# Decode step of an adaLN block: the last quarter of the gate modulation's weights as 112 rows in four pieces of 28 on partitions 0 to 27, instead of 100 rows in five pieces of 20 on partitions 32 to 51

## The chip, the cores and the metric

The kernel runs on one core of one Trainium2 chip. The time is device microseconds of one execution of the whole program; three runs of the kernel before gave 696.67, 697.14 and 704.57 us, median 697.14 us. Times inside an execution come from one profiled execution and count from its first instruction.

## The reference

One token for each of two sequences (B = 2) goes through a block whose shifts, scales and gates come from a condition vector `c` (2 x 512). Attention has 32 heads of width 128 over a cache of 4096 keys and values in float32; the feed-forward part is 512 -> 1376 -> 512 with Mish.

```python
mod = (_silu(c) @ w_mod).reshape(c.shape[0], 6, 1, -1)
sa, ca, ga, sb, cb, gb = (mod[:, 0], mod[:, 1], mod[:, 2], mod[:, 3], mod[:, 4], mod[:, 5])
h = _layernorm(x, axis=-1) * (1 + ca) + sa
x = x + ga * _A_ref(h, A_k_cache, A_v_cache, A_wq, A_wo)
h = _layernorm(x, axis=-1) * (1 + cb) + sb
x = x + gb * _B_ref(h, B_w1, B_b1, B_w2)
```

The change concerns `gb`, the sixth modulation, called m5 in the kernel: `silu(c)` (2 x 512) times the last 512 x 512 block of `w_mod`. It is needed only for the last product of the kernel.

## The kernel before

All of the cache and all weights, some 297 MB, are read once. The host lays them out as a list of "loads", each at most 128 partitions x 64 KB, in the order in which they are used (`stream`). `load(n)` puts load n into one of three rotating 64 KB-wide tiles ("room") with one or more transfers, all issued from the SP queue; `used(...)` marks a part as consumed and issues the next load once everything in the room's former load is consumed. SP's transfers take eight completion semaphores (DMAHW0 to DMAHW7) in turn, and SP's order shows that a transfer waits for the one eight places ahead of it.

For each head VectorE multiplies the keys by q and sums (lines 334 and 337), ScalarE takes exponentials, TensorE multiplies by the values. After the last head comes a tail that TensorE leads: the last values, the output projection, the second normalisation, modulations 4, 3 and 5, the two feed-forward products, and the store. In the tail every engine works through its instructions in the order of the code. The last two loads are:

- load 34: modulation 4's weights and the last head's values (3072 KB, 1024 KB, 1024 KB), then the pieces of m5, `m5p`, as four small transfers (line 154).
- load 35, seven transfers: modulation 3's weights with the first half of `w1` (2400 KB), the second half of `w1` (1376 KB), **m5's first 384 rows together with the first chunk of `w2` (1024 KB)**, then the other chunks of `w2` (1280, 768, 256 and 256 KB).

The 512 contraction rows of m5 are dealt out three ways. Rows 0 to 383 are three full blocks of 128 rows (`wm5`), in the third transfer of load 35. `PIECES` pieces of `ROWS` rows come as `m5p` with load 34: the pieces lie side by side in the free dimension, so that one partition's row holds one row of each piece, and the four transfers take every fourth row. The rest, 28 rows, lies in the padding of `w2`'s first chunk from partition 96 on (`REST0`). The matching entries of `silu(c)` are in `ct5`, one column group for each piece.

`terms5` lists the products in this order: the pieces, the three full blocks, the rest. `modulation_5(lo, hi)` issues terms lo to hi - 1, four matmuls each (one for each 128 columns), which all add into `gps`. It is called four times in the tail, among other matmuls:

```python
    modulation_5(0, 2)
...
    modulation_5(2, 4)
...
    modulation_5(4, PIECES)
...
    modulation_5(PIECES, len(terms5))
```

The third call stands between the transposition of the normalised x (`h2ps`, line 253, copied to `h2t` by VectorE) and the first feed-forward product (`w1ps`, line 560). The fourth stands behind the matmuls that add the hidden values into `fps` (line 575). `busy(n)` issues matmuls whose result is not used. VectorE then forms Mish from `fps` (lines 588 to 595), TensorE multiplies by `w2` (`yps`, line 604), and VectorE multiplies by `gb`, adds x (lines 611 and 612) and SP stores.

Of the kernel before, what the change touches and what calls it, by code (L numbers as in the profile page):

```python
# [13 lines left out]
P = 128  # L14
WIDTHS = (384, 384, 352, 256)
CHUNKS = [(g, j) for j in range(3) for g in range(4) if WIDTHS[g] > P * j]
ROW0, ROWS, STEP = 32, 20, 4
PIECES = 5
M5 = 3
REST0 = WIDTHS[2] - 2 * P  # L20
REST = 512 - P * M5 - ROWS * PIECES
HEADS = 32
HC = 4
BIG = 8192
# [3 lines left out]
    "k": BIG, "v": HALF, "wq": W, "wo": W, "m01": 2 * W, "m2": W, "m3": W, "m4": W, "m5": 512 * M5,  # L28
    "m5p": 512 * PIECES, "w1": 4 * sum(WIDTHS), "w2": 512 * len(CHUNKS),
}  # L30
# [5 lines left out]
def stream():  # L36


    order, n_v = [], 0
    for h in range(1, HEADS):  # L40
        order.append(("k", h))
        if h % HC == HC - 1 and HC < h < HEADS - 1:
            c = (h + 1) // HC
            order.append([("wq", c), ("wo", c - 2)])
        if h not in AHEAD:
            order += [("v", n_v, 0), ("v", n_v, 1)]
            n_v += 1
    order = [x if isinstance(x, list) else [x] for x in order]

    def size(x):  # L50
        return sum(SIZES[key[0]] for key in x)

    loads = [[([("m01", 0), ("wq", 0), ("wq", 1)], (4 * W,)), ([("k", 0)], (BIG,))]]
    for _ in range(1, HEADS):
        row = []
        while size(row) < ROW:
            room = ROW - size(row)
            row += order.pop(next(i for i, x in enumerate(order) if size(x) <= room))
        loads.append([(row, (ROW,))])
    last = [("v", h, i) for h in range(HEADS - 4, HEADS) for i in range(2)]  # L60
    assert order == [[key] for key in last[:2]], order
    loads += [
        [(last[:2] + [("wo", 6), ("wo", 7), ("m2", 0)], (BIG + 3 * W,))],
        [(last[2:4], (BIG,)), (last[4:6], (BIG,))],
        [([("m4", 0)] + last[6:], (W + HALF, W, W)), ([("m5p", 0)], (512 * PIECES,))],
        [
            ([("m3", 0), ("w1", 0)], (W + 2 * sum(WIDTHS), 2 * sum(WIDTHS))),
            ([("m5", 0), ("w2", 0)], (512 * (M5 + 1), 5 * 512, 3 * 512, 512, 512)),
        ],
    ]  # L70
    return loads
# [3 lines left out]
def kernel(  # L75
# [17 lines left out]
    nc = tc.nc  # L93
# [13 lines left out]
    NCH = len(CHUNKS)  # L107
    NP5 = PIECES + 1

# [14 lines left out]
    def take(t, keys):  # L124
        lo = 0
        for key in keys:
            kind, n = key[:2]
            part = t[:, lo : lo + SIZES[kind]]
            lo += SIZES[kind]
            if kind == "k":  # L130
                k_t[n] = part.rearrange("p (j d) -> p j d", d=DH)
            elif kind == "v":
                v_t[n, key[2]] = part.rearrange("p (c n) -> p c n", n=512)
            elif kind in ("wq", "wo"):
                (wq_t if kind == "wq" else wo_t)[n] = part.rearrange("p (k n) -> p k n", k=G)
            else:
                w_t[kind] = part.rearrange("p (k n) -> p k n", k={"w2": NCH, "m5": M5, "m5p": PIECES}.get(kind, G))

    w_t = {}
    done = set()  # L140

    def load(n):

        t = kvp.tile([P, ROW], F32, tag="room", name=f"room{n}", bufs=3)
        lo = 0
        for keys, srcs in loads[n]:
            take(t[:, lo:], keys)
            for src in srcs:
                dst = t[:, lo : lo + src.shape[-1]]
                if src.shape[0] == P:  # L150
                    nc.sync.dma_start(out=dst, in_=src)  # L151
                else:
                    for i in range(STEP):
                        nc.sync.dma_start(out=dst[ROW0 + i : ROW0 + ROWS : STEP], in_=src[i::STEP])
                lo += src.shape[-1]

    loaded = 0

    def used(*keys):
# [26 lines left out]
        out=fold, in_=ident.rearrange("p (g r) -> p r g", g=G), axis=AX.X, op=ALU.add  # L186
# [3 lines left out]
        out=mean_w, in0=fold[:, None, :].to_broadcast([P, G, R]), scalar1=1.0 / D, scalar2=None, op0=ALU.mult  # L190
# [4 lines left out]
        out=half, in_=ident.rearrange("p (b r) -> p r b", b=B), axis=AX.X, op=ALU.add  # L195
# [14 lines left out]
    ct5 = const.tile([P, NP5, R], F32, name="ct5")  # L210
# [99 lines left out]
    def busy(n, bank=1):  # L310

        for lo in range(0, n, 2):
            cols = P * min(2, n - lo)
            nc.tensor.matmul(ov[bank][:, :cols], lhsT=ident, rhs=e_t[0].rearrange("p c m -> p (c m)")[:, :cols], start=True, stop=True)  # L314
# [129 lines left out]
    for h in range(H):  # L444
# [38 lines left out]
        out=ct5[:, :, ::TB],  # L483
# [29 lines left out]
    wm3, wm5 = w_t["m3"], w_t["m5"]  # L513
    w1_t, w2_t = w_t["w1"], w_t["w2"]
    gps = ov[1 - N % 2][:, :P]
    rows5, rest5 = slice(ROW0, ROW0 + ROWS), slice(REST0, REST0 + REST)
    terms5 = [(ct5[rows5, n, :], w_t["m5p"][rows5, n, :]) for n in range(PIECES)]
    terms5 += [(ct[:, k, :], wm5[:, k, :]) for k in range(M5)]
    terms5.append((ct5[rest5, PIECES, :], w2_t[rest5, 0, :]))

    def modulation_5(lo, hi):
        for n in range(lo, hi):
            c, w = terms5[n]
            for g in range(G):
                nc.tensor.matmul(
                    gps[R * g : R * (g + 1)], lhsT=c, rhs=w[:, P * g : P * (g + 1)],
                    start=(n == 0), stop=(n == len(terms5) - 1),
                )
# [21 lines left out]
    nc.vector.tensor_copy(h2t[:, :, ::TB], h2ps)  # L550

    busy(1)
    modulation_5(4, PIECES)
    hq_pad = work.tile([P, 512], F32, tag="o", name="hq_pad")
    nc.gpsimd.memset(hq_pad[:, : NJ * P], 0.0)
    w1ps = wide_ps("w1ps")
    for k in range(G):
        lo = 0
# [9 lines left out]
    lo = 0  # L568
    for g in reversed(range(G)):
# [3 lines left out]
        lo = hi  # L573
    for j in range(NJ):
# [5 lines left out]
            stop=(j == NJ - 1),  # L580
            skip_group_check=True,
        )
    modulation_5(PIECES, len(terms5))
    busy(2)
    f = const.tile([P, 3, NJ * G, B], F32, name="f")
    hid = fps.rearrange("p (n b) -> p n b", b=B)
# [13 lines left out]
    for n in range(NCH):  # L600
        i = (n - 1) % NCH
# [15 lines left out]
def _lay_out(np, a):  # L617


    def rows(w):  # L620

        return w.reshape(-1, P, w.shape[-1]).transpose(1, 0, 2)

    def q_rows(v):

        return v.reshape(2, 4, P).transpose(1, 0, 2).reshape(8, P)

    B, H, S, DH = a["A_k_cache"].shape
    kv = {
        kind: a[n].reshape(B, H, P // B, -1).transpose(1, 0, 2, 3).reshape(H, P, -1)  # L630
        for kind, n in (("k", "A_k_cache"), ("v", "A_v_cache"))
    }
    wq = rows(a["A_wq"]).reshape(P, 4, 8, 512).transpose(2, 0, 1, 3).reshape(8, P, -1)
    wo = a["A_wo"].reshape(8, 4, P, 512).transpose(0, 2, 1, 3).reshape(8, P, -1)
    wm = rows(a["w_mod"])
    w1 = rows(a["B_w1"])
    starts = np.cumsum((0,) + WIDTHS)
    b1c = np.zeros((P, 12 + 2 * (PIECES + 1)), a["B_b1"].dtype)
    m5 = a["w_mod"][:, 512 * 5 :]
    m5p = np.zeros((P, PIECES, 512), m5.dtype)  # L640
    for n in range(PIECES + 1):
        f0 = P * M5 + ROWS * n
        to, size = (ROW0, ROWS) if n < PIECES else (REST0, REST)
        b1c[to : to + size, 12 + 2 * n : 14 + 2 * n] = a["c"].reshape(2, 512)[:, f0 : f0 + size].T
        if n < PIECES:
            m5p[to : to + size, n] = m5[f0 : f0 + size]
    w2 = np.zeros((P, len(CHUNKS), 512), a["B_w2"].dtype)
    for n, (g, j) in enumerate(CHUNKS):
        f0 = starts[g] + P * j
        f1 = min(f0 + P, starts[g + 1])  # L650
        b1c[: f1 - f0, n] = a["B_b1"][f0:f1]
        w2[: f1 - f0, (n + 1) % len(CHUNKS)] = a["B_w2"][f0:f1]
    w2[REST0 : REST0 + REST, 0] = m5[512 - REST :]

    pieces = {**kv, "wq": wq, "wo": wo, "m01": [wm[:, :, :1024]], "w1": [w1], "w2": [w2], "m5p": [m5p], "m5": [rows(m5)[:, :M5]]}
    for n in (2, 3, 4):
        pieces[f"m{n}"] = [wm[:, :, 512 * n : 512 * (n + 1)]]
    def piece(kind, n, part=None):
        row = pieces[kind][n].reshape(P, -1)
        return row if part is None else row[:, HALF * part : HALF * (part + 1)]  # L660

    arrays = {
        "head": np.stack([q_rows(a["c"]), q_rows(a["A_x"])], axis=1),
        "b1c": b1c,
    }
    for n, parts in enumerate(stream()):
        for i, (keys, widths) in enumerate(parts):
            row = np.concatenate([piece(*key) for key in keys], axis=1)
            cuts = np.split(row, np.cumsum(widths)[:-1], axis=1)
            for j, t in enumerate(cuts):  # L670
                arrays[f"load{n}_{i}_{j}"] = np.ascontiguousarray(t[ROW0 : ROW0 + ROWS] if keys == [("m5p", 0)] else t)
    return arrays


# [26 lines left out]
```

## Time and profile before

| what | value |
|---|---|
| times of three runs | 697.14, 696.67, 704.57 us |
| profiled execution, span from first to last instruction | 695.1 us |
| median of the runs less that span | 2.0 us |
| VectorE busy | 588.2 us (85%) |
| TensorE busy (matmul) | 290.5 us (42%) |
| ScalarE busy | 44.2 us (6%) |
| HBM read | 297.17 MB, 428 GB/s over the span |
| chain that ended last | DMA 67%, VectorE 30%, TensorE 2% |

The profiled execution is not one of the three timed runs; its own time is known only as its span, 695.1 us. The page gives busy time by engine and 40 slices of the span, the chain of work that ended last, groups of instructions and transfers. The timeline names for each instruction or run of equal instructions its start, its length, and in brackets how long the engine had been idle before it and who ended that. A line such as "1024.0 KB, 14.5" under transfers means that a transfer of that size landed 14.5 us after SP began to issue it. "PEclk" is the granted clock of TensorE as a share of full speed.

### The profile page before, as it was taken

To read this page: it belongs to the slowest core of one execution; us is meant where nothing else is said; L and a number is where in the kernel's file an instruction comes from. 1 tells how busy PE (TensorE), PEld (TensorE's weight loads), DVE (VectorE), ACT (ScalarE), POOL (GpSimd) and SP (SyncE) were. 2 spreads that over 40 slices of the span, in tenths; PEclk is the share of its full clock that TensorE was granted. 3 is DMA by queue.
4 is the path that set the end of the run, shared out by engine and by line. 5 is a ranking of instruction groups with operands and counts; after the bars stand their busy time and mean duration, and the time that the engine had idled before them with its cause. 6 is when DMAs were issued, how large, how long until landed. Compare 5 with 4: busy or idle time off the path is not lost.

```text
span 695.1 us, 4042 instructions
## 1 busy us (share of the span) xinstructions
PE 290.5 (42%) x1696; PEld 109.5 (16%) x1696; DVE 588.2 (85%) x223; ACT 44.2 (6%) x169; POOL 4.4 (1%) x20
## 2 busy tenths in 40 slices
PE   3603334335135625225242806235324425134887
PEld 1201011001002201101110301011101111001345
DVE  3599989999999999999999999999999999899002
ACT  1000000000000000000000000000000010000011
POOL 2000000000000000000000000000000000000000
PEclk9955655668575567666575565656585657656899
DMA  9999999999999999999999999999999999999997
GB/s 382 464 422 422 422 431 471 419 423 430 426 457 430 423 434 427 437 445 423 430 437 426 446 430 426 437 431 441 430 426 424 449 434 437 427 421 429 426 418 302
DMA packets 6986, 297.49 MB, mean 428 GB/s; under 512 B 924, under 2 KB 1060, under 8 KB 1444
## 3 DMA queue, kind: packets, MB, share of 16 engines
q1 hardware_dynamic: 6808, 297.22, 99.1%
q8 instruction: 13, 0.21, 0.1%
q10 hardware_dynamic: 160, 0.02, 0.0%
q14 instruction: 5, 0.04, 0.0%
HBM read 297.17 MB, written 0.07 MB: 428 GB/s over the span
## 4 chain that ended last, share of the span: by engine, by line
DMA 67%; DVE 30%; PE 2%; SPq 0%; issue 0%; ACT 0%; DVEq 0%
DMA room<-in_load 67%; DVE room L334 15%; DVE s L337 15%; PE qps L307 1%; PE modps L263 1%; SPq L151 0%; DVE m L350 0%; DVE hcw L296 0%; PE hps L253 0%; ACT q L308 0%; PE yps L604 0%; DVE y L611 0%; DVE hq L287 0%; DVE hq L286 0%; DVE y L612 0%
## 5 line engine op out<-in xcount | busy, mean ns | idle before, releaser
L334 DVE TENSOR_TENSOR room<-room,q 128x8192 f32<-128x8192 f32 x32 | 278.1, 8692 | 46.4 <-DMA room<-in_load 39.1
L337 DVE TENSOR_REDUCE s<-room 128x64 f32<-128x8192 f32 x32 | 277.9, 8684 | 0.4 <-DVE m L350 0.3
L375 PE MATMUL ov<-room,e 128*32 128x512 f32 x1024 | 170.6, 820 | 69.3 <-ACT e L353 39.8
L346 PE MATMUL mt<-d,same 128*128 128x64 f32 x64 | 19.0, 393 | 197.4 <-DVE d L344 197.4
L375 PEld LDWEIGHTS ov<-room,e 128*32 128x32 f32 x1024 | 38.4, 143 | 173.6 <-issue 125.2
L353 ACT ACTIVATE e<-s,m 64x64 f32<-64x64 f32 x64 | 22.1, 345 | 552.1 <-DVE m L350 551.3
L346 PEld LDWEIGHTS mt<-d,same 128*128 128x128 f32 x64 | 13.7, 267 | 226.3 <-DVE d L344 179.1
L307 PE MATMUL qps<-room,hcw 128*128 128x512 f32 x64 | 46.8, 902 | 4.4 <-DMA room<-in_load 3.6
L361 PE MATMUL l<-l,ones 128*128 128x8 f32 x16 | 4.6, 358 | 76.1 <-ACT e L353 76.1
L398 PE MATMUL otp<-pick,o 128*128 128x8 f32 (+2 forms) x72 | 14.4, 328 | 36.3 <-ACT o L390 34.9
L307 PEld LDWEIGHTS qps<-room,hcw 128*128 128x128 f32 x64 | 18.2, 297 | 28.0 <-issue 22.4
L398 PEld LDWEIGHTS otp<-pick,o 128*128 128x128 f32 x72 | 13.6, 282 | 45.3 <-ACT o L390 45.2
L390 DVE COPY o<-ov 128x256 f32<-128x256 f32 x1 | 0.4, 424 | 23.1 <-ACT o L390 23.1
L361 PEld LDWEIGHTS l<-l,ones 128*128 128x128 f32 x16 | 3.8, 297 | 77.5 <-ACT e L353 77.5
L350 DVE TENSOR_REDUCE m<-mt 128x1 f32<-128x64 f32 x32 | 7.0, 218 | 6.6 <-PE mt L346 6.6
L406 PE MATMUL att<-room,ot 128*32 128x512 f32 x62 | 10.2, 718 | 5.2 <-DMA room<-in_load 4.7
L353 ACT ACTIVATION_READ_ACCUMULATOR e<-s,m 64x1 f32 x64 | 11.8, 185 | 0.0
L344 DVE TENSOR_SCALAR d<-half,m 128x64 f32<-128x64 f32 x32 | 8.1, 254 | 1.1
L314 PE MATMUL ov<-e,ident 128*128 128x256 f32 (+1 forms) x36 | 8.5, 372 | 0.0
L342 DVE TENSOR_REDUCE m<-s 128x1 f32<-128x64 f32 x32 | 7.0, 217 | 0.9
L263 PE MATMUL modps<-room,ct 128*32 128x128 f32 (+1 forms) x128 | 7.0, 364 | 1.4 <-DMA room<-in_load 1.4
L390 ACT COPY o<-ov 128x512 f32<-128x512 f32 (+1 forms) x9 | 5.0, 561 | 27.3 <-PE ov L375 27.2
(107 smaller groups left out, 70.8 us busy)
## 6 DMA issues: line engine op xcount, KB each, us to landing
room<-in_load SPq DMA_DIRECT2D x4, 4096.0 KB, 25.1
room<-in_load SPq DMA_DIRECT2D x1, 7168.0 KB
room<-in_load SPq DMA_DIRECT2D x1, 3072.0 KB, 26.2
room<-in_load SPq DMA_DIRECT2D x3, 1024.0 KB, 28.3
room<-in_load SPq DMA_DIRECT2D x1, 2400.0 KB, 13.9
room<-in_load SPq DMA_DIRECT2D x1, 1376.0 KB, 14.5
room<-in_load SPq DMA_DIRECT2D x1, 1280.0 KB, 15.1
room<-in_load SPq DMA_DIRECT2D x1, 768.0 KB
```

Source lines behind the costliest of these rows:

```text
L263: nc.tensor.matmul(ps[R * g : R * (g + 1)], lhsT=ct[:, k, :], rhs=t[:, k, :].rearrange("p (m n) -> p m n", m=n)[:, :, P * g : P * (g + 1)] ...
L307: nc.tensor.matmul(ps, lhsT=hcw[:, k, :], rhs=wq_t[ch][:, k, :], start=(k == 0), stop=(k == G - 1))
L314: nc.tensor.matmul(ov[bank][:, :cols], lhsT=ident, rhs=e_t[0].rearrange("p c m -> p (c m)")[:, :cols], start=True, stop=True)
L334: nc.vector.tensor_tensor(out=k_t[h], in0=k_t[h], in1=qv, op=ALU.mult)
L337: nc.vector.tensor_reduce(out=s_t[h], in_=k_t[h], axis=AX.X, op=ALU.add)
L344: nc.vector.tensor_scalar(out=d, in0=half, scalar1=m_t[h][:, 0:1], scalar2=None, op0=ALU.mult)
L346: nc.tensor.matmul(mps[h], lhsT=same, rhs=d, start=True, stop=True)
L353: nc.scalar.activation(e_t[i][own_b, :, M * i + 4 * b : M * i + 4 * b + 4], s_t[h][own_b].rearrange("p (c m) -> p c m", m=4), AF.Exp, bias ...
L361: nc.tensor.matmul(lps[n], lhsT=ones, rhs=sum_t[n % 2], start=True, stop=True)
L375: nc.tensor.matmul(ov[bank][R * g : R * (g + 1), :], lhsT=e_t[h % HC][:, NB // 2 * part + c, :], rhs=v_t[h, part][:, c, :], start=(first a ...
L398: nc.tensor.matmul(tps[:, x], lhsT=o_t[m], rhs=pick_t[n][:, m, x], start=(m == 0), stop=(m == 3),)
L406: nc.tensor.matmul(att[R * i : R * (i + 1), :], lhsT=ot_t[n % 2][:, i, :], rhs=wo_t[n][:, i, :], start=(n == 0), stop=(n == H // HC - (2 i ...
```

## The change: what it does

There are four pieces of 28 rows instead of five of 20. They lie on partitions 0 to 27 instead of 32 to 51. Each of the four transfers now takes seven rows of 8 KB (4 x 512 floats) instead of five rows of 10 KB, so 112 rows and 224 KB come with load 34 instead of 100 rows and 200 KB. The rest is 16 rows instead of 28, in the same place in `w2`'s padding. The third and fourth calls of `modulation_5` now split the list of terms at `PIECES + 1`, which is 5 as `PIECES` was before.

```diff
-ROW0, ROWS, STEP = 32, 20, 4
-PIECES = 5
+STEP = 4
+PIECES, ROWS = 4, 28
...
-REST = 512 - P * M5 - ROWS * PIECES
+REST = 512 - P * M5 - PIECES * ROWS
...
-                dst = t[:, lo : lo + src.shape[-1]]
-                if src.shape[0] == P:
+                rows, width = src.shape
+                dst = t[:rows, lo : lo + width]
+                if rows == P:
                     nc.sync.dma_start(out=dst, in_=src)
                 else:
                     for i in range(STEP):
-                        nc.sync.dma_start(out=dst[ROW0 + i : ROW0 + ROWS : STEP], in_=src[i::STEP])
-                lo += src.shape[-1]
+                        nc.sync.dma_start(out=dst[i::STEP], in_=src[i::STEP])
+                lo += width
...
-    rows5, rest5 = slice(ROW0, ROW0 + ROWS), slice(REST0, REST0 + REST)
-    terms5 = [(ct5[rows5, n, :], w_t["m5p"][rows5, n, :]) for n in range(PIECES)]
+    rest5 = slice(REST0, REST0 + REST)
+    terms5 = [(ct5[:ROWS, n, :], w_t["m5p"][:ROWS, n, :]) for n in range(PIECES)]
     terms5 += [(ct[:, k, :], wm5[:, k, :]) for k in range(M5)]
     terms5.append((ct5[rest5, PIECES, :], w2_t[rest5, 0, :]))
...
     busy(1)
-    modulation_5(4, PIECES)
+    modulation_5(4, PIECES + 1)
     hq_pad = work.tile([P, 512], F32, tag="o", name="hq_pad")
...
-    modulation_5(PIECES, len(terms5))
+    modulation_5(PIECES + 1, len(terms5))
     busy(2)
...
-    m5p = np.zeros((P, PIECES, 512), m5.dtype)
+    m5p, f0 = np.zeros((P, PIECES + 1, 512), m5.dtype), P * M5
     for n in range(PIECES + 1):
-        f0 = P * M5 + ROWS * n
-        to, size = (ROW0, ROWS) if n < PIECES else (REST0, REST)
+        to, size = (REST0, REST) if n == PIECES else (0, ROWS)
         b1c[to : to + size, 12 + 2 * n : 14 + 2 * n] = a["c"].reshape(2, 512)[:, f0 : f0 + size].T
-        if n < PIECES:
-            m5p[to : to + size, n] = m5[f0 : f0 + size]
+        m5p[to : to + size, n] = m5[f0 : f0 + size]
+        f0 += size
```

Lines below the changed part of `load` stand one line further down after the change (604 becomes 605). How the instructions stand is shown at three places. On TensorE in the tail, between the transposition and the first feed-forward product (`room_1227` is load 34, `room_1356` load 35; the name in brackets is what an instruction waits for), before:

```order
L253 MATMUL h2ps<-ident,hq 128x8 [waits DVE_49]
L314 MATMUL ov_110<-e_160,ident 128x128
L525 MATMUL ov_109<-room_1227,ct_104 32x128 x4
L560 MATMUL w1ps<-room_1356,h2t 32x384 [waits DVE_49,Activation_49]
```

and with the change:

```order
L254 MATMUL h2ps<-ident,hq 128x8 [waits DVE_49]
L315 MATMUL ov_110<-e_160,ident 128x128
L526 MATMUL ov_109<-room_1356,ct 32x128 [waits DMAHW7_49]
L526 MATMUL ov_109<-room_1356,ct 32x128 x3
L561 MATMUL w1ps<-room_1356,h2t 32x384 [waits DVE_49,Activation_49]
```

The four matmuls of the fifth piece, which read load 34, are gone from this place; the four of the first full block stand there, read load 35 and wait for a transfer, DMAHW7. Behind `fps`, in the same queue, before:

```order
L575 MATMUL fps<-ident,hq_pad 128x8 [waits Activation_49]
L525 MATMUL ov_109<-room_1356,ct 32x128 [waits DMAHW7_49]
L525 MATMUL ov_109<-room_1356,ct 32x128 x11
L525 MATMUL ov_109<-room_1356,ct_104 32x128 x4
L314 MATMUL ov_110<-e_160,ident 128x256
L604 MATMUL yps<-room_1356,actt 32x128 [waits DVE_49,PE_49]
```

and with the change:

```order
L576 MATMUL fps<-ident,hq_pad 128x8 [waits Activation_49]
L526 MATMUL ov_109<-room_1356,ct 32x128 x8
L526 MATMUL ov_109<-room_1356,ct_104 32x128 x4
L315 MATMUL ov_110<-e_160,ident 128x256
L605 MATMUL yps<-room_1356,actt 32x128 [waits DVE_49,PE_49]
```

Four matmuls fewer stand there, and the wait for DMAHW7 has moved to the place above. On SP, the pieces and what follows them, before:

```order
L154 DMA room34_1227<-in_load34_1_0 5x2560 x2
L154 DMA room34_1227<-in_load34_1_0 5x2560 [waits DMAHW3_49]
L154 DMA room34_1227<-in_load34_1_0 5x2560 [waits DMAHW4_49]
L151 DMA room35_1356<-in_load35_0_0 128x4800 [waits DMAHW5_49,PE_49]
L151 DMA room35_1356<-in_load35_0_1 128x2752 [waits DMAHW6_49]
L151 DMA room35_1356<-in_load35_1_0 128x2048 [waits DMAHW7_49]
```

and with the change:

```order
L155 DMA room34_1227<-in_load34_1_0 7x2048 x2
L155 DMA room34_1227<-in_load34_1_0 7x2048 [waits DMAHW3_49]
L155 DMA room34_1227<-in_load34_1_0 7x2048 [waits DMAHW4_49]
L152 DMA room35_1356<-in_load35_0_0 128x4800 [waits DMAHW5_49,PE_49]
L152 DMA room35_1356<-in_load35_0_1 128x2752 [waits DMAHW6_49]
L152 DMA room35_1356<-in_load35_1_0 128x2048 [waits DMAHW7_49]
```

Only the shape of the four small transfers has changed. The last row is the transfer of m5's full blocks; it takes DMAHW7, for which TensorE waits above.

More of the change, by code (lines that the diff above doesn't have):

```diff
@@ L652, in _lay_out @@
         w2[: f1 - f0, (n + 1) % len(CHUNKS)] = a["B_w2"][f0:f1]
-    w2[REST0 : REST0 + REST, 0] = m5[512 - REST :]
-    pieces = {**kv, "wq": wq, "wo": wo, "m01": [wm[:, :, :1024]], "w1": [w1], "w2": [w2], "m5p": [m5p], "m5": [rows(m5)[:, :M5]]}
+    w2[REST0 : REST0 + REST, 0] = m5p[REST0 : REST0 + REST, -1]
+    pieces = {**kv, "wq": wq, "wo": wo, "m01": [wm[:, :, :1024]], "w1": [w1], "w2": [w2], "m5p": [m5p[:, :-1]], "m5": [rows(m5)[:, :M5]]}
     for n in (2, 3, 4):
@@ L670, in _lay_out @@
             for j, t in enumerate(cuts):
-                arrays[f"load{n}_{i}_{j}"] = np.ascontiguousarray(t[ROW0 : ROW0 + ROWS] if keys == [("m5p", 0)] else t)
+                arrays[f"load{n}_{i}_{j}"] = np.ascontiguousarray(t[:ROWS] if keys == [("m5p", 0)] else t)
     return arrays
```

## The prediction

> **What bounds the kernel now.** I read the page first, for the share of each resource.
>
> ```profile
> span 695.1 us, 4042 instructions
> DMA 67%; DVE 30%; PE 2%; SPq 0%; issue 0%; ACT 0%; DVEq 0%
> HBM read 297.17 MB, written 0.07 MB: 428 GB/s over the span
> ```
>
> The transfers run from end to end at 428 GB/s. VectorE's 30% of the chain are only the places where SP waits for a free room while earlier loads are still in flight. The change touches nothing until the last load, so all it can move is the end. There I read the chain of waits in order of time:
>
> ```profile
> 675.51 16.84 DMA room<-in_load
> 692.35 0.04 issue
> 692.39 0.47 PE yps L604 x8
> 692.88 0.30 DVE y L611
> ```
>
> The kernel ends when the last transfer of load 35 lands (692.35); after it come eight matmul passes, two steps of VectorE and the store. So TensorE's tail is not the bound now. How near it is to being the bound is what decides this change, and the timeline of the tail shows it:
>
> ```profile
> 682.64 0.47 PE L314 MATMUL ov<-e,ident 128*128 128x128 f32 x2
> 682.83 0.17 DVE L550 COPY h2t<-h2ps 128x8 f32<-128x8 f32 x1 [0.86 <-PE h2ps L253]
> 683.04 0.42 PE L525 MATMUL ov<-room,ct 20*32 20x128 f32 x8
> 683.39 2.78 PE L560 MATMUL w1ps<-room,h2t 128*32 128x384 f32 x32
> 686.73 0.84 PE L575 MATMUL fps<-ident,hq_pad 128*128 128x8 f32 x6 [0.56 <-ACT hq_pad L572]
> 687.49 1.21 PE L525 MATMUL ov<-room,ct 128*32 128x128 f32 x32
> 688.63 0.70 PE L314 MATMUL ov<-e,ident 128*128 128x256 f32 x2
> 688.93 0.20 DVE L595 TENSOR_TENSOR actt<-f 128x22 f32<-128x22 f32 x1
> 689.27 1.52 PE L604 MATMUL yps<-room,actt 96*32 96x128 f32 x48
> 691.13 1.08 PE L604 MATMUL yps<-room,actt 128*32 128x128 f32 x32 [0.34 <-DMA room<-in_load]
> 692.39 0.43 PE L604 MATMUL yps<-room,actt 128*32 128x128 f32 x8 [0.17 <-DMA room<-in_load]
> ```
>
> A matmul of the program appears as two passes (x8 for four). `yps` waits for transfers only 0.34 + 0.17 us in all. TensorE is thus about half a microsecond ahead of the transfers, and a delay beyond that anywhere from `w1ps` on reaches the end nearly in full.
>
> **The change, part by part.**
>
> *The moved term.* The third call of `modulation_5` issues term 4. That was the fifth piece, which came with load 34; now it is the first full block, whose weights are in the third transfer of load 35 (1024 KB). The order of the changed kernel has the wait for that transfer there. When it lands:
>
> ```profile
> room<-in_load SPq DMA_DIRECT2D x1, 1024.0 KB, 14.5
> 671.64 0.33 SPq L151 DMA_DIRECT2D room<-in_load  x1
> ```
>
> 671.64 + 14.5 = 686.14. That matmuls start at once after a landing is seen at load 35's first transfer, issued at 666.46 and landed 13.9 later, at 680.36, with modulation 3 starting at 680.40:
>
> ```profile
> room<-in_load SPq DMA_DIRECT2D x1, 2400.0 KB, 13.9
> 666.46 0.35 SPq L151 DMA_DIRECT2D room<-in_load  x1
> 680.40 1.08 PE L263 MATMUL modps<-room,ct 128*32 128x128 f32 x32 [0.24 <-DMA room<-in_load]
> ```
>
> So TensorE, which today runs this place at 683.04, would stand until 686.14 + 0.04 = 686.18. Everything behind it in its queue stands too: `w1ps`, `fps`, `yps`. ScalarE's `hq_pad` copies and VectorE's Mish wait for those. `h2t` is ready at 683.00 and no longer sets anything.
>
> *The pieces' transfers.* They are 25 KB more in total, 0.06 us at 428 GB/s. What counts is how they lie on the DMA engines, which no row shows: the page lists the four transfers without a landing.
>
> ```profile
> room<-in_load SPq DMA_DIRECT2D x4, 50.0 KB
> ```
>
> Bounds: 428 GB/s over 16 engines is 26.8 GB/s for one. If each transfer puts one row on each of five engines now and on each of seven then, an engine that carries pieces today gets 4 x 8 KB instead of 4 x 10 KB, 1.22 us instead of 1.53, and is 0.3 us earlier with all that follows; two engines that carry none today become 1.2 us later. A transfer lands with its slowest engine, so load 35's landings move by -0.3 (the slowest carries pieces today) to +1.2 us (the slowest is one of the two). I take -0.3: today's extra 1.5 us lie on a few engines while all other transfers load all engines alike, so the last one is likeliest among those. The Trainium skill, "DMA: Bandwidth & Descriptors", section "Why a DMA increments its semaphore by 16 and not by 1", has a transfer run on the largest number of engines up to 16 that divides its slowest dimension: five rows on five engines, seven on seven, the lowest-numbered; no row here shows it, and by it the two cases above are the only ones. SP issues the pieces in the same places with the same waits, and load 35's later transfers queue behind many microseconds of data, so their issue costs nothing; if the cover went, 0.3 us each.
>
> *The sum at TensorE's present pace.* Release at 686.18 - 0.3 = 685.88. The four moved matmuls take 683.39 - 683.04 = 0.35, so `w1ps` starts at 686.23, 2.84 later than now. From `w1ps` to `yps` it is 689.27 - 683.39 = 5.88 us; in it are now four matmuls fewer (8 of 32 passes of 1.21 us, 0.3 us), but they lay beside Mish, which ends with line 595 at 689.13, so I take 0 off. `yps` starts at 692.11. By then the last transfer has landed (692.35 - 0.3 = 692.05), and its 88 passes run without waits: 1.52 + 1.08 + 0.43 = 3.03, to 695.14 instead of 692.82. That is +2.3 us. If the landings moved by +1.2 instead it would be +3.8.
>
> *The clock.* The new wait is 685.88 - 683.11 = 2.8 us of idle TensorE. In consecutive stretches of 3.41 us the profile shows what idle time does to the granted clock (the number behind the count):
>
> ```profile
> core 0: us, PE busy (x), PEclk, DMA share, GB/s
> 649.44:652.86 3.42, 1.62 (x19) 1.00 1.02 429
> 652.86:656.27 3.41, 3.41 (x20) 0.50 0.99 425
> 656.27:659.68 3.41, 3.41 (x23) 1.00 0.90 387
> 669.92:673.34 3.42, 2.34 (x20) 1.00 1.05 435
> 673.34:676.75 3.41, 2.54 (x26) 1.00 1.01 433
> 683.57:686.99 3.42, 2.86 (x35) 1.00 1.00 413
> ```
>
> A stretch with 1.62 us of work (1.8 idle) is followed by one at half clock, a stretch with 2.34 is not (1.00 in the row behind it). With the change 683.57 to 686.99 would hold 1.1 us of work: the next stretch is granted half. I assume that the stretches' position is not tied to the program. An idle of 2.8 us is split so that neither part reaches 1.8 in (1.8 - 1.0) / 3.4, about a quarter of the positions. What half clock costs, by the values' matmuls:
>
> ```profile
> 652.90:656.20 3.30, 3.30 (x20) 0.50 0.96 410
> 662.80:666.40 3.60, 3.60 (x32) 1.00 0.97 414
> ```
>
> 165 ns for a pass instead of 112, times 1.47. A slow stretch of 3.4 us lies at most on 3.4 us of `w1ps`, which then loses 3.4 x (1 - 1/1.47) = 1.1 us; where it begins earlier or later it meets idle time or the small steps, and I estimate 0.6. So 0.6 to 1.1 in three of four positions; I take 0.9. The rule in the Trainium skill, "TensorE: Matmul & The Clock Gate", section "Part 1: The HAM clock gate", halves the clock after a whole idle window of about 3.4 us. By that rule the 2.8 us would not halve it, and the sum would stay at +2.3 (rival D); this trace's 649.44 row, half idle and followed by 0.50, speaks against it, so I go by the row.
>
> *The rest.*
>
> ```profile
> 675.80 0.42 DVE L390 COPY o<-ov 128x256 f32<-128x256 f32 x1 [23.06 <-ACT o L390]
> ```
>
> Matmuls on 28 instead of 20 rows, two columns less in the small steps on `c5` before the tail, the other partitions: TensorE's passes last as long for 20 rows as for 128 (rows at 683.04 and 687.49), and behind the `c5` steps VectorE has nothing to do for 23 us. Nothing.
>
> **Total:** 2.3 + 0.9 = +3.2 us, from a span of 695.1 to 698.3. The runs' median is 697.14, 2.0 above the span; I keep that difference: 697.14 + 3.2 = 700.3 us.
>
> **The rivals.**
>
> *A, not slower: the transfers' end stays the bound.* If the moved matmuls did not wait, or the full blocks landed by 683.1 as the pieces do, only the pieces' new spread would show: -0.3 us, 696.8. For it: the chain ends with DMA today. Against: landing at 686.14 is 3.1 us after TensorE's arrival, and the slack is half a microsecond. It decides if the third transfer lands before about 683.6. 0.08.
>
> *B, slower still: half clock for the whole rest of the tail.* The first slow stretch is itself partly idle, and the clock stays at 0.50 for another. Then `w1ps` (2.78 x 0.47 = 1.3) and `yps` (3.03 x 0.47 = 1.4, as large as 3 if short passes lose the whole factor of two) and `fps` (0.84 x 0.47 = 0.4) all lose: 2.3 + 3.1 = +5.4, 702.5. It decides if the stretch after the wait holds too little work. Against: `w1ps` at half clock alone fills 4 us. 0.14.
>
> *C, a newly loaded engine is the last.* The landings move by +1.2: +3.8 at full clock, +4.7 with one slow stretch: 701.0 to 701.9. For it: two engines that end late today are enough; against: most engines carry no piece and need not be near the last. 0.12.
>
> *D, the clock stays whole.* The idle time is split between two stretches, or half a stretch of idle time is not enough: +2.3, 699.4. For it: a quarter of the positions; against: the 649.44 row. It decides if no stretch holds less than some 1.7 us of work. 0.20. The clock rule named above gives this case in every execution.
>
> My forecast (wait as reckoned, one slow stretch, 2.3 + 0.6 to 2.3 + 1.1, so 700.0 to 700.5) has 0.43; what is left, 0.03, is something unseen. The two lower of the three runs lie 0.5 us apart, so each end is widened by that, and the lower one by some more for D: 698.5 to 702.9 holds the forecast, D, C and B; A is left out below.
>
> A measurement of this kernel can tell about 2% from no change, here 14 us. No case comes near it: within 2% 0.97, slower by over 2% 0.02 (a disturbed median), faster 0.01.
>
> **What would show it.** In the timeline after: the L526 matmuls behind `h2ps` with an idle of some 2.7 us ended by DMA; `w1ps` at about 686.2; `yps` in one unbroken run of 88 passes from about 692 to 695; the last chain going from a landing at 686 through TensorE, ScalarE and VectorE, not through the last transfer. Half clock (0.50) in one stretch after 686; none would be D, two B. The pieces' spread shows in the third transfer's time to landing: 14.2 if right, up to 15.7 if C. I am wrong if `w1ps` still starts near 683.4, or if `yps` still waits for transfers.

## The result and the profile after

The changed kernel takes 700.75 us (median of 22 runs, 697.71 to 706.85), the kernel before 696.9 us (median of 22). The ratio is 1.0051, with a 95% interval of 1.0038 to 1.0065: slower by half a per cent, clear of noise, and far inside the 2%. The runs of the kernel before lie within 0.6 us of each other but for one at 704.6; those of the changed kernel spread over 4.6 us without its one at 706.9. That spread belongs to the finding.

The profiled execution of the changed kernel took 700.22 us. Its page, the span and the chain of work that ended last:

```profile
span 698.4 us, 4026 instructions
DMA 64%; DVE 30%; PE 3%; another core or an unknown queue 2%; issue 0%; ACT 0%; SPq 0%; DVEq 0%; ACTq 0%
```

The span is 3.3 us longer, and the transfers' share of the chain falls from 67% to 64%. The 2% of "another core or an unknown queue" are one piece for which the profile names no cause. It ends where ScalarE's copies `hq_pad` start, and TensorE's wait and `w1ps` lie inside it:

```profile
679.81 10.65 another core or an unknown queue
690.54 0.38 ACT hq_pad L573
```

So the chain does not show by itself what held the end up, and the timeline has to. The timeline of the changed kernel's tail, with lines answering to those shown of before:

```profile
681.02 0.47 PE L315 MATMUL ov<-e,ident 128*128 128x128 f32 x2
684.64 0.65 PE L526 MATMUL ov<-room,ct 128*32 128x128 f32 x8 [3.16 <-DMA room<-in_load]
685.07 5.33 PE L561 MATMUL w1ps<-room,h2t 128*32 128x384 f32 x32
690.96 0.83 PE L576 MATMUL fps<-ident,hq_pad 128*128 128x8 f32 x6 [0.56 <-ACT hq_pad L573]
693.51 2.61 PE L605 MATMUL yps<-room,actt 96*32 96x128 f32 x88 [0.15 <-DVE actt L596]
696.17 0.29 DVE L612 TENSOR_TENSOR y<-yps,mod 128x128 f32<-128x128 f32 x1 [2.63 <-PE yps L605]
```

The moved matmuls stand for 3.16 us until a transfer lands; `w1ps` takes 5.33 us instead of 2.78; `yps` runs in one piece and waits for no transfer. Against the kernel before, `w1ps` starts 685.07 - 683.39 = 1.7 us later, `fps` 4.2 later, `yps` 4.2 later, and line 612 (611 before) 3.3 later, because the 88 passes of `yps` no longer wait. The landing for which the matmuls stand, by the transfers' view and by SP's timeline:

```profile
room<-in_load SPq DMA_DIRECT2D x1, 1024.0 KB, 14.2
670.43 0.33 SPq L152 DMA_DIRECT2D room<-in_load  x1
```

670.43 + 14.2 = 684.63, and TensorE goes on at 684.64. The clock, in consecutive stretches of 3.41 us of the changed kernel:

```profile
core 0: us, PE busy (x), PEclk, DMA share, GB/s
680.32:683.73 3.41, 1.16 (x20) 1.00 1.01 423
683.73:687.14 3.41, 2.50 (x25) 0.50 0.98 412
687.14:690.56 3.42, 3.26 (x21) 0.50 0.54 214
690.56:693.97 3.41, 2.85 (x49) 1.00 0.00 0
```

The stretch that holds most of the wait has 1.16 us of work and is followed by two at half clock, which cover all of `w1ps`.

### The profile page after: what moved, and what is told of

It reads as the page before. It is cut to its first block, busy times and chain, and to the rows that moved or that the text cites. A ratio compares the mean times of both kernels' runs of the same rounds, so it can differ in the third digit from the quotient of the medians.

```text
span 698.4 us, 4026 instructions
## 1 busy us (share of the span) xinstructions
PE 292.7 (42%) x1688; PEld 109.5 (16%) x1688; DVE 588.2 (84%) x223; ACT 44.2 (6%) x169; POOL 4.4 (1%) x20
## 4 chain that ended last, share of the span: by engine, by line
DMA 64%; DVE 30%; PE 3%; another core or an unknown queue 2%; issue 0%; ACT 0%; SPq 0%; DVEq 0%; ACTq 0%
DMA room<-in_load 64%; DVE room L335 15%; DVE s L338 15%; PE qps L308 1%; PE modps L264 1%; PE yps L605 0%; PE ov L315 0%; PE ov L376 0%; SPq L152 0%; PE otp L399 0%; DVE m L351 0%; PE fps L576 0%; DVE hcw L297 0%; PE hps L254 0%
```

## The experiments

All times are medians; the kernel before, run beside each group, gave 696.79 to 696.91 us. Three questions: is it the moved term or the pieces' spread; how much of the loss is the wait and how much the clock; and, after the first answers, why the stream of transfers itself had become faster.

**The moved term taken back.** The first full block stands behind `fps` again; the pieces stay as changed.

```diff
-    modulation_5(4, PIECES + 1)
+    modulation_5(4, PIECES)
...
-    modulation_5(PIECES + 1, len(terms5))
+    modulation_5(PIECES, len(terms5))
```

> The changed kernel with the old place of the moved term: the third call of modulation_5 issues nothing, and the first full block stands behind fps again, as before the change. The pieces stay as the change has them (four of 28 rows, seven rows to a transfer). Theory (the wait for load 35's third transfer, with the half clock that follows it, is all of the loss): TensorE no longer waits ahead of w1ps, w1ps starts at about 683 and takes 2.8 us, the end is set by the last transfer again, and the time is 696.6 us, between 0 and 0.5 us under the kernel before. Rival (the new spread of the pieces puts load on engines that end late): the loss stays in part, 698 us or more, and yps waits for transfers at its end by over a microsecond.

Measured: 696.06 us (694.9 to 699.85, 12 runs), ratio 0.9978 (0.9951 to 1.0006). In the profiled execution (695.04 us) TensorE goes from filler to `w1ps` without a wait and at full clock:

```profile
681.08 0.47 PE L315 MATMUL ov<-e,ident 128*128 128x128 f32 x2
681.58 2.77 PE L561 MATMUL w1ps<-room,h2t 128*32 128x384 f32 x32
```

The loss is gone, so the theory of the loss holds, and its rival (newly loaded engines end late) falls as the cause of it. Two things didn't fit: the median is 0.8 us under the kernel before, where at most 0.5 was expected, and the best runs are 1.7 us under it, more than the pieces could give. And the runs spread over 5 us.

**The moved term alone,** in the kernel before with its five pieces; the third call issues the fifth piece and then the first full block.

```diff
-    modulation_5(4, PIECES)
+    modulation_5(4, PIECES + 1)
...
-    modulation_5(PIECES, len(terms5))
+    modulation_5(PIECES + 1, len(terms5))
```

> The kernel before with only the moved term: five pieces of 20 rows as before, and the third call issues the fifth piece and then the first full block, so that TensorE waits for load 35's third transfer ahead of w1ps. Theory: all of the loss is here, 700 to 701.5 us, with runs spread over 698 to 703 as those of the changed kernel are, since the position of the clock's stretches differs from run to run. Rival (the spread of the pieces is what costs): 697 us, as before.

Measured: 700.88 us (698.9 to 706.96, 12 runs), ratio 1.0055 (1.0025 to 1.0084): the whole loss, without any change to the pieces. Its timeline:

```profile
686.17 0.43 PE L525 MATMUL ov<-room,ct 128*32 128x128 f32 x8 [2.80 <-DMA room<-in_load]
686.41 4.44 PE L560 MATMUL w1ps<-room,h2t 128*32 128x384 f32 x32
```

The first pass comes at 686.17, where the prediction had 686.18 for landings that do not move. That the idle time, 2.80 us, also equals the prediction's 2.8 is chance: here the fifth piece still stands ahead of the wait, and the landing is not 0.3 us earlier. `w1ps` takes 4.44 us, and here one stretch of 3.41 us was at half clock:

```profile
683.04:686.46 3.42, 0.62 (x20) 1.00 1.01 417
686.46:689.87 3.41, 3.41 (x34) 0.50 0.91 369
689.87:693.28 3.41, 2.85 (x41) 1.00 0.19 74
```

**The wait filled with work.** Six filler matmuls (12 passes) ahead of the four that wait, in the changed kernel.

```diff
+    busy(12)
     modulation_5(4, PIECES + 1)
```

> The changed kernel with six more filler matmuls of 256 columns (12 passes, about 2.7 us) directly ahead of the four matmuls that wait, so that TensorE works through most of the wait; the wait itself stays. Theory (the loss is the wait, some 2 us, and half clock after it, some 1 to 2 us): the clock stays at 1.00 in the tail, w1ps takes 2.8 us instead of 5.3, the time is 698.6 to 699.4 us and the runs lie within 1 us of each other. Rival (the half clock costs nothing at the end, the wait is all): 700.5 us as the changed kernel, spread as before. If the clock were all of the loss: 697 us.

Measured: 698.03 us (697.2 to 700.01, 12 runs), ratio 1.0014 (0.9994 to 1.0035). Timeline and clock in that run:

```profile
681.79 3.06 PE L315 MATMUL ov<-e,ident 128*128 128x128 f32 x14
685.28 0.42 PE L526 MATMUL ov<-room,ct 128*32 128x128 f32 x8 [0.43 <-DMA room<-in_load]
685.52 2.75 PE L562 MATMUL w1ps<-room,h2t 128*32 128x384 f32 x32
```

```profile
680.32:683.73 3.41, 3.41 (x42) 1.00 1.04 437
683.73:687.14 3.41, 2.98 (x39) 1.00 0.97 402
```

TensorE gets past the wait 0.64 us later than in the changed kernel (685.28 and 684.64), but with the clock at 1.00, and `w1ps` takes 2.75. Work that computes nothing makes the kernel 700.75 - 698.03 = 2.7 us faster. The two profiled executions agree: from the start of `w1ps` to the start of `yps` (691.38 here) it is 5.86 us with the filler and 693.51 - 685.07 = 8.44 without, 2.6 more. The expectation was 0.6 too high at its lower end, because the clock costs more than I had thought, and the runs lie 2.8 us apart instead of within 1 us.

**Pieces of 32 rows,** three of them, without the early block: eight rows to a transfer. The edit is shown against the first run.

```diff
-PIECES, ROWS = 4, 28
+PIECES, ROWS = 3, 32
...
-    modulation_5(2, 4)
+    modulation_5(2, 3)
...
-    modulation_5(4, PIECES)
+    modulation_5(3, PIECES)
```

> As the run without the early block, but with three pieces of 32 rows, so that each of the four transfers takes eight rows of 6 KB (24 KB for each of eight engines, if a transfer puts one row on each, instead of 32 KB on seven), and the rest is 32 rows. Theory (the last transfer sets the end, and it is the slowest engine that ends it): 0.3 us under the run with seven rows if its slowest engine carries pieces, up to 0.9 us over it if the eighth engine is one that ends late. Rival (only the mean rate of the transfers counts): the same as the run with seven rows within 0.1 us.

Measured: 696.61 us (696.47 to 697.69, 12 runs), ratio 0.9994 (0.9975 to 1.0013), 0.5 over the run with seven rows. That is inside the theory's -0.3 to +0.9 and outside the rival's 0.1, but it shows nothing about the eighth engine, since the two runs turned out to differ in something else too.

**Where the rooms lie.** The chain of waits in order of time has one row that can be compared between all kernels: the last VectorE product that waits for a landing, long before any piece is issued. Kernel before, then changed kernel:

```profile
625.37 8.69 DVE room L334
```

```profile
624.20 8.69 DVE room L335
```

The whole stream was 1.2 us ahead long before the first changed transfer; SP issues the first piece at 644.24 in the kernel before. The changed kernel's small tiles are shorter (`ct5` by 128 bytes of a partition, `bias` and a temporary by 8 each), and the three rooms are allocated behind them: in the memory map of the built kernels the first begins at byte 32640 of each partition before, 128 beyond a multiple of 256, and at 32512, a multiple of 256, with the change; the other two lie 64 KB and 128 KB behind it. Two runs tell this apart from the pieces. First the kernel before with the rooms moved, by an added tile ahead of them and one tile fewer:

```diff
+    pad = const.tile([P, 40], F32, name="pad")
...
-    f = const.tile([P, 3, NJ * G, B], F32, name="f")
+    f = hcw.rearrange("p g b -> p (g b)")[:, : 3 * NJ * G * B].rearrange("p (a n b) -> p a n b", a=3, b=B)
```

> The kernel before (five pieces of 20 rows, early block not moved) with nothing changed but where the rooms lie in SBUF: the Mish tile is put into memory that is free by then and an unused tile of 160 bytes is added, so that the rooms begin at byte 32512 of a partition, as in the changed kernel, instead of 32640 (a multiple of 256 instead of 128 beyond one). Theory formed after the first four runs (the changed kernel's stream is faster because the smaller ct5 has moved the rooms): the last head's product of VectorE starts at about 624.3 us instead of 625.4, and the time is 695.3 to 696 us. Rival (the stream is faster for another reason, such as the pieces): 696.8 us and 625.4 as in the kernel before.

Then the first run of this study with a tile of 128 bytes that moves them back:

```diff
+    pad = const.tile([P, 32], F32, name="pad")
```

> The run without the early block (four pieces of 28 rows, seven to a transfer) with an unused tile of 128 bytes added, so that the rooms begin at byte 32640 as in the kernel before. Theory: the last head's product starts at about 625.4 us again, what is left of the gain is the pieces' own 0.3 us, and the time is 696.5 us. Rival (the seven-row pieces make the whole gain): 695 to 696 us as without the tile.

Measured: rooms moved in the kernel before, 695.5 us (694.91 to 703.01, 12 runs; the ratio is 0.9989, 0.9972 to 1.0006, with the one run of 703.01 in it; the other eleven, up to 696.01, lie below every run of the kernel before beside them, 696.59 and more). Rooms moved back, 697.4 us (696.45 to 699.64, 11 runs), ratio 1.001 (1.0001 to 1.0018). The same row of the chain, for the first and the second:

```profile
624.10 8.69 DVE room L335
```

```profile
625.36 8.69 DVE room L336
```

So the row follows the rooms' place and not the pieces, in both directions. The time followed too, but the second did not stop at 696.5: with the rooms back, seven-row pieces are 0.6 us slower than the kernel before.

The eight-row pieces were then run with the rooms at 32512 (they had been at 32352, 96 beyond a multiple of 256), and with the rooms at 32256, a multiple of 512; both only add an unused tile, the second also places `f` as above.

> The run with eight-row pieces (three of 32 rows), with an unused tile of 160 bytes added, so that its rooms begin at byte 32512 instead of 32352 (96 beyond a multiple of 256). Theory: the stream is as fast as in the changed kernel (last head's product at about 624.3 us) and the time falls by about 0.8 us to 695.8; where it then stands to the run without the early block is what eight engines instead of seven are worth, within 0.6 us either way. Rival (the rooms' place is without effect): 696.6 us.

> Eight-row pieces with the rooms at byte 32256, a multiple of 512, instead of 32512, a multiple of 256 only (the Mish tile in memory free by then, an unused tile of 192 bytes). Theory (256 bytes is the step that counts): 695.6 us, as at 32512, last head's product at 624.3 us. Rival (the larger the power of two the better): 694.5 us and 623.3.

Measured: at 32512, 695.62 us (694.97 to 696.15, 11 runs), ratio 0.9979 (0.9970 to 0.9988). At 32256, 695.72 us (694.88 to 701.28, 11 runs). The row, at 32352, 32512 and 32256:

```profile
625.65 8.69 DVE room L335
```

```profile
624.28 8.69 DVE room L336
```

```profile
624.39 8.69 DVE room L336
```

Of the four places tried, the two at a multiple of 256 are fast; 512 gives nothing more. The kernel with eight-row pieces at 32512 is the one version here whose whole interval of the ratio lies below 1.

**The spread.** Fillers of 256 columns at three places of the tail were to remove the late runs of the version without the early block:

```diff
     value_sums(N % 2, (nc.scalar.copy,))
+    busy(4, 1 - N % 2)
     head_values(N, 0, HC - 1)
+    busy(2, 1 - N % 2)
     project_o(N)
...
-    modulation_5(4, PIECES)
+    busy(2)
```

> The run without the early block, with filler matmuls of 256 columns at the places where TensorE stands in the tail: one where the third call of modulation_5 was, two ahead of the last group's head values and one behind them. Theory (that run's slower executions, 696 to 700 us, are executions in which the clock was halved after idle time in the tail, since the transfers now end so early that TensorE's tail is close to the bound): 695.1 us median, with fewer runs above 696. Rival (they come from the transfers): 696 us median, spread over 695 to 700 as without filler.

Measured: 696.28 us (695.41 to 701.9, 11 runs), no better than without, which is the rival's number. But its profiled execution (695.95 us) does not point at the transfers: a stretch at half clock, from 673.1 to 676.5, still falls at the start of the tail, the last eight passes of the values take 1.91 us instead of the 1.07 of the first run, and `yps` then runs in one piece without a wait.

```profile
673.06 1.91 PE L376 MATMUL ov<-room,e 128*32 128x512 f32 x8 [1.21 <-DMA room<-in_load]
689.34 2.61 PE L607 MATMUL yps<-room,actt 96*32 96x128 f32 x88
```

So these fillers did not remove the half clock that they were meant to remove. The version without filler was profiled twice more.

> The run without the early block once more, for the profile alone, since its twelve times lay between 694.9 and 699.9 us and only one of 695.0 had a profile. If this execution takes over 696 us: theory (half clock in the tail) has a stretch at 0.50 behind 672 us and w1ps longer than 2.8 us or later than 682; rival (the transfers of the pieces, seven rows each, hold up the others) has yps waiting for its last transfers until 692 or later at full clock. If it takes 695 us it says nothing more than the first profile.

> The same kernel and the same question as the run before it: over 696 us either with a half-clock stretch behind 672 us (theory) or with the last transfers landing at 692 or later at full clock (rival).

Measured: 697.8 and 695.87 us. In the execution of 697.8:

```profile
679.50 1.40 PE L264 MATMUL modps<-room,ct 128*32 128x128 f32 x32 [0.76 <-DMA room<-in_load]
683.73 4.35 PE L561 MATMUL w1ps<-room,h2t 128*32 128x384 f32 x32
691.18 2.61 PE L605 MATMUL yps<-room,actt 96*32 96x128 f32 x88
```

```profile
676.70:680.12 3.42, 2.61 (x49) 1.00 0.96 410
680.12:683.53 3.41, 3.41 (x42) 0.50 1.03 433
683.53:686.94 3.41, 3.41 (x28) 0.50 0.98 407
```

Half clock from 680 to 687, `w1ps` 1.6 us longer, and `yps` without a wait for transfers at the end: the clock made this execution late. The execution of 695.87 was not late by the clock: from 672.3 us on it ran at full clock, and its last transfer landed at 691.39, 0.8 us later than in the execution of 695.04 (690.55). So the landings have a part in the spread too. Whether the pieces make them late is not shown: with eight-row pieces at the same rooms the last landing is at 691.16. The profiled run of the kernel before with the rooms moved happened to be its one of 703.01 us; there half clock was granted from 672.87 to 693.35, six stretches in a row, the first five full of work (all but the third and fourth of the six are shown):

```profile
669.46:672.87 3.41, 1.47 (x16) 1.00 1.00 418
672.87:676.28 3.41, 3.41 (x23) 0.50 1.01 434
676.28:679.70 3.42, 3.42 (x53) 0.50 1.00 426
686.53:689.94 3.41, 3.41 (x29) 0.50 0.66 263
689.94:693.35 3.41, 3.35 (x21) 0.50 0.01 5
693.35:696.77 3.42, 2.92 (x55) 1.00 0.00 0
```

**The changed kernel with the rooms back,** by the same tile of 128 bytes:

> The changed kernel, with the early block and its wait, and an unused tile of 128 bytes that puts the rooms back to byte 32640. Theory (the rooms' place speeds the stream, and with it the landing that TensorE waits for): the wait ends 1.1 us later than in the changed kernel's profile (685.7 instead of 684.6), and the time is 701.8 us. Rival (with TensorE's tail as the bound, the median hangs on where the half-clock stretches fall and the rooms' place is lost in that): 700.8 us, as the run of the kernel before with the early block alone, which has the rooms at the same place.

Measured: 701.28 us (698.75 to 704.01, 6 runs), ratio 1.0064 (1.0045 to 1.0084), between the two answers. In its profile the wait ends later than the 685.7 expected, because the transfer took 15.2 us to land:

```profile
687.00 0.43 PE L527 MATMUL ov<-room,ct 128*32 128x128 f32 x8 [3.08 <-DMA room<-in_load]
687.24 4.44 PE L562 MATMUL w1ps<-room,h2t 128*32 128x384 f32 x32
```

With six runs five microseconds apart the median doesn't decide.

## Why the prediction was right, and where its terms were wrong

700.3 us was forecast and 700.75 measured, inside 698.5 to 702.9. The mechanism was the one named: the first and second run show that the moved term makes the loss, and the third that the clock is a large part of it. That the total is so near is partly luck: two terms were off by over a microsecond, in opposite directions. In steps that the runs allow, each against the one above it:

| step | median, us | difference |
|---|---|---|
| kernel before | 696.9 | |
| rooms at a multiple of 256 | 695.5 | -1.4 |
| four pieces of 28 rows | 696.06 | +0.6 |
| wait ahead of `w1ps`, clock kept up by filler | 698.03 | +2.0 |
| filler gone: half clock behind the wait | 700.75 | +2.7 |

- *The moved term* was right: its place, the transfer that it waits for, and that everything behind it in TensorE's queue and the two engines that feed on it stand too. TensorE went on at 684.64 instead of 685.88 because the stream was ahead.
- *The sum at TensorE's present pace*, +2.3, measured +2.0 with the clock kept up, against the version without the wait and with the rooms at the same place. That version has late runs of its own: against the kernel before with the rooms moved it is +2.5, and between the two profiled executions, both at full clock from 672 us on, VectorE's last instruction starts 694.37 - 691.41 = 3.0 later. So the term is 2 to 3 us. From `w1ps` to `yps` it took 5.86 us at full clock, where 5.88 was reckoned, and `yps` ran unbroken, as reckoned.
- *The clock* was the mis-sized term: 0.9 forecast, 2.7 measured. "Times 1.47", from the values' matmuls, was the wrong row for `w1ps`, which at half clock takes 5.33 against 2.78, 1.92 times as long. And I had taken one slow stretch; the profiled execution has two. The two others with the wait (the term alone, the rooms back) have one, and `w1ps` loses 4.44 - 2.78 = 1.7 us there, still more than the 1.1 that was reckoned at most. The prediction's rival B had this mechanism with 5.4 us, which was too much, since the clock was back at 1.00 before `yps`. The Trainium skill, "TensorE: Matmul & The Clock Gate", section "Part 1: The HAM clock gate", asks for a whole idle window of about 3.4 us before the clock falls; here it fell behind stretches with 1.16 and 1.47 us of work, and once behind one with 2.61, so the trace disagrees with the page. My own reading of the rows, a limit at some 1.7 us of work, does not hold either: 2.61 us made of 49 short passes was not enough, 2.54 was in the kernel before, and in the execution of 703.01 five stretches full of work were each followed by another at half clock. What a stretch must hold stays open.
- *The rest, "nothing"*, and with it "the change touches nothing until the last load", failed for the small tiles: shortening them moved the rooms, worth -1.4 us. I had costed the instructions on `ct5`, not what is allocated behind it.
- *The pieces' spread*: -0.3 forecast. The third transfer's time to landing, 14.2 us, was to show it, and the changed kernel's profile has just that; but this is chance too. Over the eight profiled executions with seven-row pieces it is 13.7 to 15.2 us (15.2 with the rooms back), and with five rows 14.4 or 14.5, so neither -0.3 nor rival C's 15.7 can be read from it. The fastest runs of the seven-row version (694.9) are no faster than those of five rows at the same rooms (694.91), and its median is 0.6 slower, with the rooms at 32512 as at 32640. One of its late executions was half clock; whether the others were too, and why its runs spread more than those of the five-row and eight-row versions, stays open.
- *Rivals A, C and D*: A fell (TensorE's tail is the bound); C fell with the first run as an account of the loss. D is not what the profiled executions with the wait show: all three (changed kernel, term alone, rooms back) have a `w1ps` of 4.44 us or more. The fastest timed runs with the wait, 697.7 to 698.9, have no profile and may be D.

## What to carry to other kernels

A list of terms split by a count keeps its length when the count changes, but not what stands at each place: look up which transfer each matmul of an in-order queue reads, because one early wait holds all behind it. A wait of 3 us on TensorE cost 2 to 3 us directly and 2.7 through the clock, so work that computes nothing can pay inside such a wait. When a small tile changes size, look where the large transfer targets behind it have moved.

## What the runs showed of the hardware that I had not expected

Transfers into rooms at a multiple of 256 bytes of the partition brought the stream to its last head 1.2 us earlier (624.1 to 624.5 against 625.4 to 625.7 in the row shown), about 0.2% of the stream, for an unchanged order of transfers; between 96 and 128 bytes beyond a multiple of 256 (625.7 against 625.4 to 625.6) there is no difference clear of the spread. The Trainium skill, "DMA: Bandwidth & Descriptors", section "How a descriptor splits into AXI transactions", says of reads that each of the transactions into which a transfer is cut must start at a multiple of 256 bytes, so that a read which begins off such a boundary costs more. The rooms are written, not read, by these transfers, and no run here shows the transactions; whether the same holds for writes is not shown.
